# Six float32 products of the identity stand in TensorE's queue among the first scores

## Chip, cores and metric

One core of a Trainium2 chip runs the whole program in one launch. The metric is the device time of one execution in microseconds (us), as the median of the runs. TensorE is called PE here, VectorE DVE, ScalarE ACT, GpSimd POOL, and SP is the queue that issues most of the transfers.

## What is computed

An attention layer with a memory term, and behind it a stack of matrix products. Cut to what matters:

```
B, H, S, D = 4, 8, 576, 64
scores = (q @ k^T) / sqrt(D); causal mask; softmax          # a
local  = a @ v
q_p    = elu(q) + 1
mem    = (q_p @ M_prev) / (q_p . z_prev + 1e-6)
g      = sigmoid(beta) per head
attn   = g * mem + (1 - g) * local
x      = attn as (B*S = 2304, H*D = 512)
out    = ((x @ w1) * (x @ w2)) @ w3 @ w_out                 # 512 -> 1024 -> 1024 -> 512
```

All arrays are float32.

## The kernel before

The attention is worked off in 16 units, each a batch and two heads (`unit_step`). A unit's scores are made in blocks of 128 query rows (`s_all`, line 250; `s_mm0`, line 233), and DVE takes each block out of PSUM, adds the mask and finds the row's extreme in one instruction (`s_red`, line 221). ACT makes the exponentials (`s_exp`, line 265), DVE or ACT scales the rows by their sums (`s_norm`, lines 270 to 278), PE transposes the rows (`t_mm`, line 289), ACT copies them (line 314), and PE multiplies them with v (`pv_mm`, line 326). Line 351 on ACT and line 352 on DVE put the unit's result into the tiles `xs`. The memory term has its own small chain: ACT at lines 172 and 173, DVE at line 179, a product with z (line 181, on DVE in some units and on POOL in others), a sum on DVE (line 189), and a scaling (line 203).

Since nothing stands between `@ w3` and `@ w_out`, the kernel multiplies these two weights with each other first, once. The weights come in as 64-bit words that ACT (line 369) and DVE (lines 373 and 374) turn into float32; the converted tiles are called `wo` (of w_out) and `hh` (of w3). The weight product has eight blocks of 128 rows, each the sum of eight PE products of 128 x 512 (`w_gen`, line 493). Blocks 0 and 1 are made side by side in the two PSUM tiles named `m`; from block 2 on each block takes one of the same two tiles when it is free. A finished block is rounded by ACT into `wH` (line 498), and DVE writes the remainder into `wL` (line 485); after that the PSUM tile is free. So the first product of block 2, which this text calls the third block, waits for the line 485 of block 0. Later the stack of products runs on PE (lines 545 and 566).

The order of the work is written by hand, as the strings in `ORDERS`, one for each unit and one ahead of the first. A word is a step: `ss` and `s0` are the scores, `e0` to `e4` exponentials, `n2` to `n4` normalisations, `ma`, `mv` and `md` the memory term, `gg` the gate of sigmoid values (`gate`), `c` one tick of the weight conversion, `F1` and so on so many weight products. Underneath, a scheduler of the tile framework decides the order in which instructions stand on each engine, by its own idea of how long each takes and of what is ready; the strings give it priorities. An instruction put in at one place can therefore move others far behind it. Each engine works its queue strictly in the order that results.

`warm(n)` can put n transposes of the identity into PE's queue. Before, it is called with n = 0 alone, where it only hands out the PSUM tile of the gate.

Of the kernel before, what the change touches and what calls it, by code (L numbers as in the profile page):

```python
# [20 lines left out]

LOADS = "q0 r1 be r3 n0 r6"
ORDERS = (
    1 * ["ss s0 e2 e1 gg e0 F3 e3 c lq F1 c n3 ma n2 F3 c mv lv lqn F2 md e4 n4 F2"]
    + 1 * ["t1 t2 t3b t4b ma c c ts t4a t3a F1 th pv fin s0 c mb ss e4 c e2 F1 lv F1 e0 F3 c F2 md F3 lq lqn F1 e1 e3 F2 n2 n3 a4"]
    + 1 * ["ma ts t2 t1 t3a t4b th t4a t3b pv fin lv ss e4 e1 s0 mb lq e3 e2 mc n3 lqn e0 a4 n2"]
    + 1 * ["t4b t1 F2 t3b c F2 ma ts th t4a t3a F3 t2 pv mv fin F1 ss e2 c c e3 s0 F1 e1 n3 lqn e4 e0 c md F2 lq lv n2 F2 a4"]
# [14 lines left out]
def attention_moe_kernel(  # L42
# [13 lines left out]
    nc = tc.nc  # L56
# [30 lines left out]
    ident = const.tile([128, 128], F32, name="ident")  # L87
# [27 lines left out]
    def split_qk(p):  # L115
        t = raw_t[p]
        hi = s4_p.tile([128, 2, 640], F32R, tag="s4", name="hi")
        lo = s4_p.tile([128, 2, 640], F32R, tag="s2", name="lo")
        parts_t[p] = hi, lo
        for o, n in ((0, 320), (320, S)):  # L120
            x, y, z = (i[:, :, o:n] for i in (t, hi, lo))
            nc.scalar.activation(out=y, in_=x, func=ACTF.Copy)  # L122
            nc.vector.tensor_tensor(out=z, in0=x, in1=f32(y), op=ALU.subtract)  # L123
# [13 lines left out]
    def load_v(w):  # L137
        p, (c0, c1) = units[w]
        b, h = heads(p)
        t = v_p.tile([128, 2, 4, D], F32, tag="v", name="v")  # L140
        u = v_p.tile([128, 5, 2, D], F32, tag="u", name="u")
        v_t[w] = t, u
        y = v[b, h:h + 2].rearrange("h p k d -> p h k d")
        nc.sync.dma_start(out=t[:, :, 0:c1 - 1], in_=y[:, :, 0:c1 - 1])
        for a in range(2):
            nc.sync.dma_start(out=u[0:64, c0:c1, a], in_=v[b, h + a][0:64, c0:c1])
        m = m_prev[b][:, h:h + 2]
        nc.sync.dma_start(
            out=u[64:128, c0:c1].rearrange("p c a d -> p c (a d)"),
            in_=bass.AP(tensor=m.tensor, offset=m.offset, ap=[[DM, D], [0, c1 - c0], [1, 2 * D]]),  # L150
        )

    def load_qn(w):
        p, (c0, c1) = units[w]
        b, h = heads(p)
        t = qn_p.tile([128, 5, 2, D], F32, tag="qn", name="qn")
        y = qn[b, h // 2]
        nc.sync.dma_start(out=t[64:128, c0:c1], in_=y[0:64, c0:c1])
        k = max(c0, 1)
        nc.sync.dma_start(out=t[0:64, k:c1], in_=y[64:128, k - 1:c1 - 1])  # L160
        if c0 == 0:
            nc.sync.dma_start(out=t[0:64, 0], in_=y[0:64, 0])
        zt = z_p.tile([128, 2, D], F32, tag="z", name="z")
        zs = z_prev[b, h:h + 2]
        nc.sync.dma_start(out=zt, in_=bass.AP(tensor=zs.tensor, offset=zs.offset, ap=[[0, 128], [D, 2], [1, D]]))
        qn_t[w], z_t[w] = t, zt
# [118 lines left out]
    def t_mm(w, what):  # L285
        p, (c0, c1) = units[w]
        pt = pts(w)
        ps = bank()
        tr = lambda o, c, a, kc: nc.tensor.transpose(ps[:, o:o + 128], sm(p, a, c)[:, 128 * kc:128 * kc + 128], ident)  # L289
        if what in ("4a", "4b", "3a", "3b"):  # L290
            c, a = int(what[0]), "ab".index(what[1])
            for kc in range(4):
                tr(128 * kc, c, a, kc)
            s = 256 if c == 4 else 0
            o = 128 if c == 4 else 256
            d = pt[:, a, s:s + 1536].rearrange("p (k q) -> p k q", q=384)[:, :, o:o + 128]
            job = (ps.rearrange("p (k q) -> p k q", q=128), d)
        elif what == "h":
            nc.tensor.transpose(ps[:, 0:128], sm0, ident)
            job = (ps[:, 0:128].rearrange("p (a q) -> p a q", a=2), pt[:, :, SP[0]:SP[0] + 64])  # L300
        else:
            blocks, lo, st, o = {
                "1": (((1, 0), (1, 1)), 0, SP[1], 0),
                "2": (((2, 0), (2, 1)), 0, 384, 128),
                "s": (((2, 2), (4, 4)), 1024, 384, 256),
            }[what]
            here = [i for i, (c, kc) in enumerate(blocks) if c0 <= c < c1]
            k0, k1 = here[0], here[-1] + 1
            for a in range(2):
                for i in here:  # L310
                    tr(256 * a + 128 * i, blocks[i][0], a, blocks[i][1])
            d = pt[:, :, lo:lo + 2 * st].rearrange("p a (k q) -> p a k q", q=st)[:, :, k0:k1, o:o + 128]
            job = (ps.rearrange("p (a k q) -> p a k q", a=2, q=128)[:, :, k0:k1], d)
        nc.scalar.activation(out=job[1], in_=job[0], func=ACTF.Copy)  # L314
# [157 lines left out]
    early = []  # L472

    def warm(n=4):
        if not early:
            early.extend(ps_m.tile([128, DM], F32, tag="m", name="m") for _ in range(2))
        for _ in range(n):
            nc.tensor.transpose(early[0][:, 0:128], ident, ident)
        return early[1]

    def w_gen():
# [136 lines left out]
    def try_tick():  # L618
        if tick[0] <= NJ + 1 and tick_ok():
            conv_tick()  # L620

    def unit_step(w, F):
        p, (c0, c1) = units[w] if w >= 0 else (0, (0, 0))
        nx = w + 1 < NU
        n0, n1 = units[w + 1][1] if nx else (9, 9)
        pn = units[w + 1][0] if nx else NP
        n2 = w + 2 < NU
        here = lambda c: c0 <= c < c1
        then = lambda c: n0 <= c < n1

        ops = dict(
            lqn=(n2, lambda: load_qn(w + 2)),
            lv=(nx, lambda: load_v(w + 1)),
            t4a=(here(4), lambda: t_mm(w, "4a")),
            t4b=(here(4), lambda: t_mm(w, "4b")),
            t3a=(here(3), lambda: t_mm(w, "3a")),
            t3b=(here(3), lambda: t_mm(w, "3b")),
            t2=(here(2), lambda: t_mm(w, "2")),
            t1=(here(1), lambda: t_mm(w, "1")),
            th=(here(0), lambda: t_mm(w, "h")),  # L640
            ts=(w >= 0, lambda: t_mm(w, "s")),
            sh=(nx, lambda: split_qk(pn)),
            ss=(nx, lambda: s_all(w + 1)),
            s0=(then(0), lambda: s_mm0(pn)),
            e4=(then(4), lambda: s_exp(w + 1, 4)),
            e3=(then(3), lambda: s_exp(w + 1, 3)),
            e2=(then(2), lambda: s_exp(w + 1, 2)),
            e1=(then(1), lambda: s_exp(w + 1, 1)),
            e0=(then(0), lambda: s_exp(w + 1, 0)),
            n3=(then(3), lambda: s_norm(w + 1, 2, 4)),  # L650
            n2=(then(0), lambda: s_norm(w + 1, 4, 9)),
            n4=(then(4), lambda: s_norm(w + 1, 0, 2)),
            a4=(then(4), lambda: s_norm(w + 1, 0, 2, True)),
            a3=(then(3), lambda: s_norm(w + 1, 2, 4, True)),
            lq=(n2, lambda: load_qk(w + 2)),
            pv=(w >= 0, lambda: pv_mm(w)),
            fin=(w >= 0, lambda: fin(w)),
            ma=(nx, lambda: mem_a(w + 1)),
            mb=(nx, lambda: mem_b(w + 1, nc.gpsimd)),
            mv=(nx, lambda: mem_b(w + 1, nc.vector)),  # L660
            mc=(nx, lambda: mem_c(w + 1, nc.gpsimd)),
            md=(nx, lambda: mem_c(w + 1, nc.vector)),
            gg=(1, gate),
        )
        for t in ORDERS[w + 1].split():
            if t[0] == "F":
                F.slot(int(t[1:] or 0) * 870)
            elif t == "c":
                try_tick()
            elif t == "d":  # L670
                warm()
            elif ops[t][0]:
                ops[t][1]()

    def gate():
        x = warm(0)[:, 0:H]
        nc.tensor.matmul(x, lhsT=ident[0:1, 0:1].to_broadcast([1, 128]), rhs=beta_sb[0:1], start=True, stop=True)
        nc.scalar.activation(out=g_sb, in_=x, func=ACTF.Exp, scale=-1.0)
        nc.scalar.activation(out=gi, in_=x, func=ACTF.Exp)
        nc.vector.tensor_scalar(out=g_sb, in0=g_sb, scalar1=1.0, scalar2=None, op0=ALU.add)  # L680
        nc.vector.reciprocal(out=g_sb, in_=g_sb)
        nc.vector.tensor_scalar(out=gi, in0=gi, scalar1=1.0, scalar2=None, op0=ALU.add)
        gp = gi.rearrange("p (j a) -> p j a", a=2)
        for k in range(4):
            nc.vector.tensor_copy(out=gis[:, :, 2 * k:2 * k + 2], in_=gp)
        for a in range(2):
            nc.vector.tensor_copy(out=gis[64 * a:64 * a + 64, :, 8], in_=gp[64 * a:64 * a + 64, :, a])
# [18 lines left out]
    for w in range(-1, NC):  # L706
        unit_step(w, F)
# [43 lines left out]
```

## Time and profile before

| | before |
|---|---|
| median of 3 runs | 537.77 us (537.25 to 538.07) |
| profiled execution, its own time | 536.97 us |
| its span, first to last instruction | 535.2 us |
| mean granted clock of PE | 0.997 |
| PE busy | 517.8 us (97%) |
| PE's weight loads busy | 393.9 us (74%) |
| ACT busy | 305.0 us (57%) |
| DVE busy | 289.4 us (54%) |
| POOL busy | 70.5 us (13%) |
| read from HBM | 46.14 MB |

The busy shares are means over the whole span. The start is another thing than the rest: there PE has gaps, the transfer engines are full, and DVE and ACT work without a break. So the stretches of the start are to be read one by one. A granted clock of 1.00 is 2.4 GHz, one of 0.50 is 1.2 GHz.

### The profile page before, as it was taken

How to read it: one execution, taken by the hardware profiler on the slowest of the kernel's cores; microseconds unless marked ns; L12 is line 12 of the kernel's file. 1: busy time of each engine (PE TensorE's matmuls, PEld its weight loads, DVE VectorE, ACT ScalarE, POOL GpSimd, SP SyncE). 2: the span in 40 equal slices, each digit the busy share in tenths (PEclk: the TensorE clock that was granted, in tenths of full speed). 3: DMA queues.
4: the chain of work that ended last, by engine and by line, in shares of the span. 5: the costliest groups of instructions: out<-in, count | busy, mean ns of one | idle time of the engine just before them, and what ended most of it. 6: DMA issues, size and time to landing. Idle time of an engine off the chain costs nothing.

```text
span 535.2 us, 8570 instructions
## 1 busy us (share of the span) xinstructions
PE 517.8 (97%) x3090; PEld 393.9 (74%) x3090; DVE 289.4 (54%) x898; ACT 305.0 (57%) x709; POOL 70.5 (13%) x92
## 2 busy tenths in 40 slices
PE   3999997999999999999999999999999999999997
PEld 2455553557878788778887878787878788888995
DVE  5989789997846476359282758282526111111110
ACT  5689799869567557286575667475747301111121
POOL 1001111000011023001110322010104300114012
PEclk9899999999999999999999999999999999999999
DMA  8998488143303031304030414031210000001001
GB/s 313 417 326 274 116 271 273 39 140 106 116 7 114 14 100 51 129 26 119 8 112 9 130 43 136 23 93 29 61 35 31 35 26 0 0 1 59 21 1 39
DMA packets 34587, 51.40 MB, mean 96 GB/s; under 512 B 13170, under 2 KB 25714, under 8 KB 31986
## 3 DMA queue, kind: packets, MB, share of 16 engines
q1 hardware_dynamic: 34402, 50.74, 29.3%
q8 instruction: 24, 0.39, 0.3%
q14 instruction: 17, 0.14, 0.1%
q10 hardware_dynamic: 144, 0.13, 0.1%
HBM read 46.14 MB, written 4.72 MB: 95 GB/s over the span
## 4 chain that ended last, share of the span: by engine, by line
PE 85%; DVE 6%; ACT 5%; DMA 2%; issue 1%; POOL 0%; SPq 0%; ACTq 0%; DVEq 0%; POOLq 0%
PE m L545 38%; PE m L566 19%; PE x L326 9%; PE s L289 8%; PE s L250 5%; PE m L493 4%; PE sx L250 2%; DMA qn<-qn 1%; ACT s L265 1%; DVE s L221 1%; ACT pt L314 1%; DMA raw<-qkt 1%; ACT wsp L381 1%; DVE sm L221 1%; DVE s L278 1%
## 5 line engine op out<-in xcount | busy, mean ns | idle before, releaser
L545 PE MATMUL m<-xs,wsp 128*128 128x512 f32 (+1 forms) x1008 | 213.4, 365 | 0.0
L545 PEld LDWEIGHTS m<-xs,wsp 128*128 128x128 f32 x1008 | 166.7, 189 | 27.7 <-issue 0.2
L566 PE MATMUL m<-wH,hs 128*128 128x512 f32 x288 | 95.7, 401 | 0.0
L314 ACT ACTIVATE pt<-s 128x512 f32<-128x512 f32 (+1 forms) x128 | 64.0, 558 | 29.2 <-PE s L289 25.2
L265 ACT ACTIVATE s<-s,mx 128x320 f32<-128x320 f32 (+2 forms) x96 | 56.2, 588 | 35.0 <-DVE mx L221 34.9
L527 POOL TENSOR_TENSOR hs<-hh,hs 128x512 fp32r<-128x512 f32 (+1 forms) x41 | 47.6, 1161 | 210.9 <-ACT hs L526 208.9
L554 DVE SCALAR_TENSOR_TENSOR hh<-m,hh 128x512 f32<-128x512 f32 (+1 forms) x40 | 25.5, 637 | 75.5 <-PE m L545 73.8
L493 PE MATMUL m<-wo,hh 128*128 128x512 f32 x128 | 60.4, 616 | 5.0 <-DVE hh L374 4.5
L566 PEld LDWEIGHTS m<-wH,hs 128*128 128x128 f32 x288 | 54.2, 188 | 12.2
L566 PE MATMUL m<-wL,hs 128*128 128x512 f32 x144 | 56.8, 394 | 0.0
L552 ACT ACTIVATE hh<-m 128x512 f32<-128x512 f32 (+1 forms) x40 | 22.0, 551 | 55.9 <-PE m L545 55.5
L493 PEld LDWEIGHTS m<-wo,hh 128*128 128x128 f32 x128 | 23.5, 194 | 31.9 <-issue 23.0
L289 PE MATMUL s<-ident,s 128*128 128x128 f32 x320 | 43.4, 274 | 2.6 <-DVE s L278 1.7
L289 PEld LDWEIGHTS s<-ident,s 128*128 128x128 f32 x320 | 36.7, 140 | 11.1 <-DVE s L278 2.5
L526 ACT ACTIVATE hs<-hh 128x512 fp32r<-128x512 f32 (+1 forms) x41 | 23.7, 577 | 36.5 <-DVE hh L554 18.3
L326 PE MATMUL x<-pt,v 128*64 128x512 f32 (+3 forms) x256 | 38.0, 439 | 0.2 <-ACT pt L314 0.2
L123 DVE TENSOR_TENSOR lo<-raw,hi 128x640 fp32r<-128x640 f32 (+1 forms) x24 | 18.3, 778 | 33.2 <-ACT hi L122 31.6
L352 DVE TENSOR_TENSOR xs<-x,xs 128x576 fp32r<-128x576 f32 (+6 forms) x24 | 13.3, 556 | 42.2 <-ACT xs L351 42.2
L221 DVE CUSTOM_DVE_ANT_0 s<-s,mask 128x320 f32<-128x320 f32 (+1 forms) x64 | 24.4, 420 | 21.9 <-PE sx L250 16.5
L351 ACT ACTIVATE xs<-x 128x576 fp32r<-128x576 f32 (+6 forms) x24 | 11.7, 489 | 39.8 <-PE x L326 35.8
L326 PEld LDWEIGHTS x<-pt,v 128*64 128x64 f32 x256 | 17.0, 136 | 22.3 <-issue 16.6
L581 DVE COPY o<-m 128x512 f32<-128x512 f32 x17 | 11.7, 689 | 37.6 <-PE m L566 37.5
(87 smaller groups left out, 652.6 us busy)
## 6 DMA issues: line engine op xcount, KB each, us to landing
raw<-qkt SPq DMA_DIRECT2D x16, 576.0 KB, 3.9
wst<-w3t SPq DMA_DIRECT2D x8, 1024.0 KB, 9.2
wst<-w SPq DMA_DIRECT2D x8, 1024.0 KB, 8.3
out<-o SPq DMA_DIRECT2D x17, 256.0 KB, 2.0
wst<-w_out SPq DMA_DIRECT2D x4, 1024.0 KB, 10.2
v<-v SPq DMA_DIRECT2D x16, 256.0 KB, 2.8
qn<-qn SPq DMA_DIRECT2D x16, 160.0 KB, 4.0
u<-v SPq DMA_DIRECT2D x32, 80.0 KB, 2.5
```

The source lines that it names most:

```text
L221: nc.vector.tensor_tensor_reduce(out=sm(p, a, c)[:, lo:hi] if c else sm0[:, 0:64], in0=x, in1=mask[:, S - KE[c] + lo:S - KE[c] + hi] if c ...
L250: nc.tensor.matmul(y[a], lhsT=qq[r, 0, 128 * c - 64:128 * c + 64], rhs=kk[r, 1, l:n], start=k == 0, stop=k == len(terms) - 1,)
L265: nc.scalar.activation(out=x, in_=x, func=ACTF.Exp, bias=mx, scale=-1.0, accum_out=sums_of(w)[:, k:k + 1])
L289: tr = lambda o, c, a, kc: nc.tensor.transpose(ps[:, o:o + 128], sm(p, a, c)[:, 128 * kc:128 * kc + 128], ident)
L314: nc.scalar.activation(out=job[1], in_=job[0], func=ACTF.Copy)
L326: nc.tensor.matmul(x[64 * a:64 * a + 64, X0 + lo:X0 + hi], lhsT=vv[:, a, k] if k < 4 else uu[:, k - 4, a], rhs=pt[:, a, o + lo - z:o + hi ...
L493: nc.tensor.matmul(ps, lhsT=w[:, 128 * kc:128 * kc + 128], rhs=wo[:, 512 * (kc % 2):512 * (kc % 2) + 512], start=(kc == 0), stop=(kc == 7))
L526: nc.scalar.activation(out=hs[:, 0, f0:f1], in_=y, func=ACTF.Copy)
L527: nc.gpsimd.tensor_tensor(out=hs[:, 1, f0:f1], in0=y, in1=f32(hs[:, 0, f0:f1]), op=ALU.subtract)
L545: nc.tensor.matmul(ps[:, o:o + k], lhsT=w[:, y, x, j], rhs=xs[j][:, xx, q:q + k], start=(j == order[0] and z == 0), stop=(j == order[-1] a ...
L554: nc.vector.scalar_tensor_tensor(out=hh[:, f, 0:c], in0=ps[:, 0:c], scalar=2.0 ** -8, in1=hh[:, f, 0:c], op0=ALU.mult, op1=ALU.mult)
L566: nc.tensor.matmul(ps, lhsT=hs[:, a, f], rhs=b[f], start=(k == 0), stop=(k == 23))
```

## The change

A word `d6` ahead of the first scores calls `warm(6)`, and `warm` now issues plain float32 products of the identity with itself, 128 x 128 x 128 each, in place of transposes. They write a part of one of the two early PSUM tiles that nobody reads; the first weight product starts that tile afresh. The gate is cut in two steps, `gg` (its product and ACT's two exponentials) and `gh` (DVE's part), which stand next to each other.

```diff
-    1 * ["ss s0 e2 e1 gg e0 F3 ...
+    1 * ["d6 ss s0 e2 e1 gg gh e0 F3 ...
@@ warm
         for _ in range(n):
-            nc.tensor.transpose(early[0][:, 0:128], ident, ident)
+            nc.tensor.matmul(early[0][:, 0:128], lhsT=ident, rhs=ident, start=True, stop=True)
@@ unit_step
             gg=(1, gate),
+            gh=(1, gate_end),
         )
...
-            elif t == "d":
-                warm()
+            elif t[0] == "d":
+                warm(int(t[1:]))
@@ gate
         nc.scalar.activation(out=gi, in_=x, func=ACTF.Exp)
+
+    def gate_end():
         nc.vector.tensor_scalar(out=g_sb, in0=g_sb, scalar1=1.0, scalar2=None, op0=ALU.add)
```

Lines behind 664 move by one, and behind 679 by three. In the built program the six stand behind six score products, since the scheduler moved them, and from there on the order of several engines differs. Three places matter below.

PE's queue at the start of the program, before (`raw` is the first unit's q and k; `s` and `sx` are scores in PSUM; x2 counts equal rows):

```order
L250 MATMUL s<-raw 128x320 x2
L250 MATMUL s<-raw 128x192 x2
L250 MATMUL s<-raw 128x448 x2
L250 MATMUL sx<-raw 128x512 x2
L250 MATMUL s<-raw 128x64 x2
L233 MATMUL s<-raw 64x64 x2
L677 MATMUL m<-beta_sb,ident 128x8
L493 MATMUL m<-wo,hh 128x512 x8
```

The same place now:

```order
L250 MATMUL s<-raw 128x320 x2
L250 MATMUL s<-raw 128x192 x2
L250 MATMUL s<-raw 128x448 x2
L478 MATMUL m<-ident 128x128 x6
L250 MATMUL sx<-raw 128x512 x2
L250 MATMUL s<-raw 128x64 x2
L233 MATMUL s<-raw 64x64 x2
L678 MATMUL m<-beta_sb,ident 128x8
L493 MATMUL m<-wo,hh 128x512 x8
```

The six are ahead of the scores `sx` and all that follows, and behind the first six.

DVE's queue where the second unit's scores are worked off and block 0 of the weight product ends, before (`wL_117` and `wL_118` are `wL` of blocks 0 and 1; rows `L221 ISA mx` write the found extreme):

```order
L221 ISA sm_108,mx<-s,mask 128x448
L221 ISA mx 128x1
L352 TENSOR_TENSOR xs_125<-x,xs_125 128x64
L179 SCALAR_TENSOR_TENSOR qn<-qn,e 128x640
L485 SCALAR_TENSOR_TENSOR wL_117<-m,wH_109 128x512
L485 SCALAR_TENSOR_TENSOR wL_118<-m,wH_110 128x512
L221 ISA s_429,mx<-sx,mask 128x512
```

The same place now:

```order
L179 SCALAR_TENSOR_TENSOR qn<-qn,e 128x640
L270 SCALAR_TENSOR_TENSOR sums<-sums,gis 128x2
L271 RECIPROCAL sums<-sums 128x2
L278 TENSOR_SCALAR sm_108<-sm_108,sums 128x448
L189 TENSOR_REDUCE n<-e 128x10
L221 ISA s_435,mx<-sx,mask 128x512
L221 ISA mx 128x1
L221 ISA s_435,mx<-sx,mask 128x512
L221 ISA mx 128x1
L221 ISA s_435,mx<-s,mask,mx 128x64
L221 ISA mx 128x1
L221 ISA s_435,mx<-s,mask,mx 128x64
```

Next come `L221 ISA mx 128x1` and then the two rows of line 485: these now stand behind a scaling, a sum and four score rows that were behind them.

DVE's queue at the fourth unit, where line 179 releases POOL's product of line 181, before (`wsp` and `wp` are weights of the stack; `s_777` is a tile of scores):

```order
L382 TENSOR_TENSOR wsp<-wp,wsp 128x512
L271 RECIPROCAL sums<-sums 128x5
L271 RECIPROCAL sums<-sums 128x2
L179 SCALAR_TENSOR_TENSOR qn<-qn,e 128x640
L278 TENSOR_SCALAR s_777<-s_777,sums 128x320 x2
L278 TENSOR_SCALAR s_777<-s_777,sums 128x192 x2
L278 TENSOR_SCALAR sm_107<-sm_107,sums 128x64
```

The same line 179 now:

```order
L373 TENSOR_SCALAR wp<-wp 128x512
L374 SCALAR_TENSOR_TENSOR wp<-wst,wp 128x512
L382 TENSOR_TENSOR wsp<-wp,wsp 128x512
L179 SCALAR_TENSOR_TENSOR qn<-qn,e 128x640
L221 ISA s_783,mx<-s,mask 128x320
L221 ISA mx 128x1
L352 TENSOR_TENSOR xs_127<-x,xs_127 128x512
L221 ISA s_783,mx<-s,mask 128x320
```

Line 179 moved ahead of that unit's score rows; the four scalings of line 278 stay behind them, some 40 rows further on. Besides these, near the start one conversion of `hh` on DVE (lines 373 and 374) moved ahead of the first `sx` row, and the second half of that `hh` tile moved five scalings back.

## Rows read from the trace of the kernel before

**Rows 1.** Windows: from:to, length, busy us (instructions) of each engine, PEclk, DMA share, GB/s.

```profile
5.00:10.00 5.00, 4.41 (x26) 2.72 (x22) 3.38 (x13) 3.09 (x11) 0.00 (x0) 1.00 1.00 418
10.00:15.00 5.00, 1.14 (x2) 0.30 (x2) 4.96 (x27) 5.00 (x16) 0.00 (x0) 0.93 0.87 284
15.00:20.00 5.00, 4.44 (x8) 1.76 (x8) 5.00 (x18) 3.57 (x7) 0.00 (x0) 0.73 1.02 429
20.00:25.00 5.00, 5.00 (x17) 2.53 (x17) 5.00 (x11) 1.79 (x4) 0.00 (x0) 1.00 1.00 417
```

**Rows 2.** Chain that ended last, 0 to 60 us: start, length, what.

```profile
19.10 0.67 DVE wo L374
...
19.82 3.70 PE m L493 x8
```

**Rows 3.** A window as in rows 1, of 1 us.

```profile
15.00:16.00 1.00, 1.00 (x2) 0.51 (x2) 1.00 (x5) 1.00 (x3) 0.00 (x0) 0.50 1.03 434
```

**Rows 4.** Timeline of PE: start, length, engine, line, what, count, idle before.

```profile
7.64 1.02 PE L250 MATMUL sx<-raw 64*128 64x512 f32 x4
...
13.86 5.40 PE L493 MATMUL m<-wo,hh 128*128 128x512 f32 x8 [4.45 <-DVE hh L374]
...
15.36 1.91 PE L493 MATMUL m<-wo,hh 128*128 128x512 f32 x2
...
36.47 1.21 PE L326 MATMUL x<-pt,u 128*64 128x128 f32 x20
...
41.85 7.99 PE L493 MATMUL m<-wo,hh 128*128 128x512 f32 x18
```

**Rows 5.** Timeline of DVE, ACT and the queue SP, 9 to 17 us.

```profile
9.03 0.68 DVE L221 CUSTOM_DVE_ANT_0 s<-sx,mask 128x512 f32<-128x512 f32 x1
9.45 0.65 ACT L369 ACTIVATE hh<-wst 128x512 f32<-128x512 f32 x1
16.95 0.33 SPq L445 DMA_DIRECT2D wst<-w3t  x1
```

**Rows 6.** Timeline of DVE and POOL, 32 to 45 us.

```profile
32.58 0.49 DVE L221 CUSTOM_DVE_ANT_0 s<-s,mask 128x320 f32<-128x320 f32 x1 [0.81 <-PE s L250]
...
38.08 0.62 DVE L221 CUSTOM_DVE_ANT_0 sm<-s,mask 128x448 f32<-128x448 f32 x1 [0.51 <-PE s L250]
...
40.37 0.83 DVE L179 SCALAR_TENSOR_TENSOR qn<-qn,e 128x640 f32<-128x640 f32 x1 [0.37 <-ACT e L173]
41.11 1.28 DVE L485 SCALAR_TENSOR_TENSOR wL<-m,wH 128x512 fp32r<-128x512 f32 x2
42.31 0.68 DVE L221 CUSTOM_DVE_ANT_0 s<-sx,mask 128x512 f32<-128x512 f32 x1
...
43.52 0.28 DVE L221 CUSTOM_DVE_ANT_0 s<-s,mask,mx 128x64 f32<-128x64 f32 x1
...
43.94 0.82 DVE L189 TENSOR_REDUCE n<-e 128x10 f32<-128x640 f32 x1
...
46.32 0.45 DVE L278 TENSOR_SCALAR sm<-sm,sums 128x448 f32<-128x448 f32 x1
41.27 1.55 POOL L181 TENSOR_TENSOR e<-qn,z 128x640 f32<-128x640 f32 x1 [39.24 <-DVE qn L179]
```

**Rows 7.** Timeline of DVE and POOL: line 278 alone, and beside POOL's line 181.

```profile
17.53 1.14 DVE L278 TENSOR_SCALAR s<-s,sums 128x320 f32<-128x320 f32 x4
91.62 2.42 DVE L278 TENSOR_SCALAR s<-s,sums 128x320 f32<-128x320 f32 x4
91.92 1.76 POOL L181 TENSOR_TENSOR e<-qn,z 128x640 f32<-128x640 f32 x1 [22.00 <-DVE qn L179]
```

**Rows 8.** PE's waits, 60 to 130 us: for what, us in total, times, longest.

```profile
PE s L289 <- DVE s L278: 1.7, 1, 1.7
PE sx L250 <- DVE xs L352: 1.6, 1, 1.6
PE s L289 <- ACT s L276: 0.8, 2, 0.5
```

More of the change, by code (lines that the diff above doesn't have):

```diff
@@ L23 @@
 ORDERS = (
-    1 * ["ss s0 e2 e1 gg e0 F3 e3 c lq F1 c n3 ma n2 F3 c mv lv lqn F2 md e4 n4 F2"]
+    1 * ["d6 ss s0 e2 e1 gg gh e0 F3 e3 c lq F1 c n3 ma n2 F3 c mv lv lqn F2 md e4 n4 F2"]
     + 1 * ["t1 t2 t3b t4b ma c c ts t4a t3a F1 th pv fin s0 c mb ss e4 c e2 F1 lv F1 e0 F3 c F2 md F3 lq lqn F1 e1 e3 F2 n2 n3 a4"]
```

## The prediction

> **What bounds the kernel now.** Read the windows of the start first [rows 1]. From 5 to 20 us PE is not the bound: between 10 and 15 us it is busy for 1.14 of 5 us, while DVE is busy for 4.96 and ACT for 5.00, and the transfer engines are full (shares of 0.87 to 1.02). The chain of waits says the same: the last DVE piece of it starts at 19.10 and is a conversion of `wo`; from 19.82 the chain is PE alone [rows 2], and PE is busy without a gap, for 5.00 of 5 us from 20 to 25 [rows 1]. The waits of PE from 60 to 130 us are the third thing to read: 1.7 us for line 278 on DVE, 1.6 for `xs` and 0.8 for line 276 [rows 8], 4.1 us in all. So three things can move the end: when PE's dense stretch begins, whether a new gap opens in it, and how much of the later waits a delay is given back from.
>
> PE's clock is low in one place: 0.50, so 1.2 GHz, in the window from 15 to 16 us [rows 3], behind a gap of 4.45 us that ended at 13.86 [rows 4]. The means of 0.93 and 0.73 over 5 us each [rows 1] are 0.7 and 2.7 us at 0.50, so 3.4 us in all.
>
> **The six products.** Each is 128 columns wide. Nine products of 512 columns take 7.99 us at the full clock [rows 4], so 0.89 each, and by the columns 0.22 for one of 128: 1.33 us for six. From below: 20 pieces of 128 columns and less of line 326 take 1.21 us [rows 4], 0.06 each, and the six are twelve such pieces, 0.7 us. From above: at 0.50 one product of 512 columns takes 1.91 us [rows 4], a quarter of it six times is 2.9 us. I take 1.33, as these are the same kind of product with the same full array. They start where `sx` started, at 7.64, so `sx` ends near 10.0 and not at 8.66. Before, that would have hurt, since DVE took `sx` at 9.03 [rows 5]. Now DVE does something else there: a conversion of `hh`, then two blocks of 448, and it comes to `sx` only after 12 us. That covers the 1.33, and the 2.9 too. If DVE were earlier by 2.3 us, it would wait. Cost on the path: 0.
>
> **The early DVE order.** DVE is free at 9.03, and the conversion now standing there needs ACT's line 369, which runs from 9.45 for 0.65 [rows 5]. DVE waits until 10.10, so 1.07 us; the blocks behind it were ready. The second half of that `hh` tile, of about 0.6, stands further back, so the first weight products see only some 0.5 of it. Then DVE is late by 1.07 again, but it has waits of its own: 0.81 at 32.58, 0.51 at 38.08, 0.37 at 40.37 [rows 6], 1.69 together. By 40 us DVE is level. PE, without gaps, stays late by something like 1 to 1.7 us at 42 us, and that is hidden if PE then waits longer anyway (next part). A load on SP waits for the tile that the moved half frees. It went out at 16.95 [rows 5]; now it goes out near 21.5, and all loads on that queue behind it. The transfer engines are at 1.00 until 25 us [rows 1], working off loads issued before, so I cost this at nothing; if that backlog ends first, it is the second rival.
>
> **The third block.** Its first product starts on PE at 41.85 [rows 4], 0.10 after the first line 485 on DVE, which starts at 41.11 and takes half of 1.28 [rows 6]. This is the term that decides. Line 179 ends at 41.11 as before, and it releases POOL's line 181, from 41.27 for 1.55, to 42.82 [rows 6]. DVE now comes to a scaling of line 278 while POOL works. Such a meeting is in the trace: four scalings take 1.14 alone and 2.42 beside POOL's line 181 [rows 7]. So the scaling ends about 0.45 [rows 6] after POOL, at 43.27. Then come line 189 (0.82), the four score rows (42.31 to 43.94, so 1.63), line 485 (0.64) and the 0.10 [rows 6]: 46.46, which is 4.6 later. Rows overlap the next by 0.08 or so, so I take 4.4. Without the meeting, line 189 still waits for POOL: 46.01, so 4.2 at most and 3.8 if DVE's wait of 0.37 at 40.37 goes. From above, 4.6 and one more wait for ACT's exponential of 0.3: 4.9. PE has finished all it can do by then, its earlier lateness included, so 4.4 is the whole delay at this point.
>
> The Trainium skill, "SBUF — State Buffer", "Who interferes with whom", states that DVE and GpSimd share a port pair which one of them locks while the other blocks fully, and that a DVE instruction with one SBUF input outside the two-port modes stays clear of it. The trace agrees, with 2.42 against 1.14 us. By that rule the give-back of the next part is sure; if the meeting were chance instead, 1.28 would not return and the sum would be 3.5.
>
> **What is given back.** In the fourth unit line 179 now stands ahead of the score rows, so POOL's line 181 runs beside these and not beside the scalings. A score row takes 0.68 beside POOL, at 42.31 [rows 6], and 0.68 alone, at 9.03 [rows 5]. The 2.42 become 1.14: 1.28 us of the 1.7 that PE waits there [rows 7, 8]. The other waits are 1.6 and 0.8 [rows 8]. PE comes later, its feeders (ACT's exponentials, `xs`) come later too but by less, as they have slack; against it the new order may open a wait of about 1 us at the second unit's end. Carrying the durations of the rows through the new order leaves 0.9 given back; the ends are 0 and 2.4. Sum: 4.4 - 1.28 - 0.9 = 2.2 us.
>
> **Rivals.**
>
> 1. *All is given back.* PE's delay of 4.4 meets 4.1 us of later waits [rows 8]. If what ends these is set by ACT, DVE and loads that PE's delay does not reach, PE only waits less: 4.4 - 4.1 = 0.3, so 538.1 and not slower by a measurable amount. It decides at the waits for `xs` and for line 278: both must vanish. For it speaks that ACT and DVE have slack after 42 us. Against it, that scores are made by PE itself, so its delay reaches the feeders. Chance 0.16.
> 2. *The loads come late.* The weight tiles behind 21.5 us arrive after the backlog has ended, and nothing but the collision is given back, or not even that: up to 4.4, 542.2. Against it the full shares in rows 1. Chance 0.13.
> 3. *The clock falls in the new gap.* PE stands still from about 42.9 to 46.3. The gap ahead of 13.86 was followed by 0.50 [rows 3, 4]; with the products then taking 1.91 instead of 0.89 [rows 4], about 1.7 us are lost in a stretch like that one. 2.2 + 1.5, so 541.5. Other gaps, of 1.6 and 1.7 us [rows 8], had no fall. Chance 0.13.
> 4. *The products lift the clock and that pays.* The 3.4 us at 0.50 do the work of 1.7 [rows 1]; without them 1.7 us would be saved if PE were the bound there: 536.1. But DVE is the bound [rows 1, 2], and the clock was 1.00 already when `sx` started, so the forecast counts nothing for it. Chance 0.05.
>
> The Trainium skill, "TensorE: Matmul & The Clock Gate", Part 1, states that activity of PE releases the gate and idleness closes it; the 0.50 after the gap agrees. By that rule alone the change helps, which is rival 4.
>
> **How the numbers follow.** The profiled execution took 536.97 us (span 535.2), the median is 537.77, 0.80 above. 536.97 + 2.2 = 539.2 for a profile, and 537.77 + 2.2 = 540.0 for the median. The forecast has a chance of 0.53; its own range is 538.7 to 541.0 (from below 3.8 - 1.7 - 1.2 = 0.9 with half of the 2.4, from above 4.9 - 1.28 - 0.4 = 3.2 with half of the 0.9). The range reaches to most of rivals 1 to 3: 538.0 to 542.3. A measurement of this kernel can tell about 0.2%, 1.08 us, from no change, so 536.7 to 538.8 is the same. Faster: rival 4 and a little of rival 1, 0.07. The same: most of rival 1 and the low end of the forecast, 0.18. Slower: 0.75.
>
> **What would show it.** The six at about 0.22 us each, from 7.6 to 9.0 us. DVE waiting about 1 us near 9 us for ACT's line 369. The third block's first product near 46.3, after a PE gap of some 3.5 us that line 485 ends. Four scalings of the fourth unit at about 1.1 us, and no 1.7 us wait for them. PE's clock at 1.00 from 46 on. The prediction is wrong if DVE reaches line 485 before 43 us, if PE's gap ends later than 47, or if the later waits are nearly gone or unchanged.

## The result, and the profile after

The changed kernel takes 542.18 us (median of 4 runs, 540.94 to 542.53), the kernel before 537.51 us beside it (537.05 to 538.07): a ratio of 1.0081, 95% interval 1.0066 to 1.0096. The profiled execution took 542.15 us, its span is 540.4 us against 535.2. The prediction had the direction and the place right, and 542.18 lies at the top of its range (538.0 to 542.3). That it lies inside, by 0.12, is luck: the same kernel took 542.80 the next time. The likeliest time was 540.0: the loss is about twice what the prediction called likeliest, and more than half of what is missing is a mechanism that it had put aside as a rival.

TensorE (PE) at the start and around the third block, kernel after: start, length, engine, line, what, count of records, idle time before and what ended it.

```profile
4.46 3.57 PE L250 MATMUL s<-raw 64*128 64x320 f32 x12 [4.46 <-DMA raw<-qkt]
7.96 2.41 PE L478 MATMUL m<-ident 128*128 128x128 f32 x12
...
12.10 1.13 PE L493 MATMUL m<-wo,hh 128*128 128x512 f32 x2
16.54 8.03 PE L493 MATMUL m<-wo,hh 128*128 128x512 f32 x14 [3.32 <-ACT e L172]
...
42.32 1.98 PE L493 MATMUL m<-wo,hh 128*128 128x512 f32 x4
46.99 9.69 PE L493 MATMUL m<-wo,hh 128*128 128x512 f32 x18 [2.69 <-DVE wL L485]
...
64.20 1.89 PE L250 MATMUL s<-raw 64*128 64x320 f32 x12
```

The row of 46.99 is the one to set beside the last of [rows 4]. The third block starts at 46.99 and not at 41.85, so 5.14 us later; and its 18 records take 9.69 us and not 7.99, so 1.70 us longer. Windows of the same stretch, kernel after (columns as in rows 1), show why they take longer:

```profile
44.00:46.00 2.00, 0.30 (x1) 0.00 (x0) 2.00 (x6) 1.12 (x3) 0.00 (x0) 1.00 0.97 386
46.00:48.00 2.00, 1.01 (x2) 0.50 (x3) 2.00 (x9) 1.83 (x5) 0.00 (x0) 0.80 1.28 259
48.00:50.00 2.00, 2.00 (x4) 0.84 (x3) 2.00 (x11) 1.96 (x5) 0.00 (x0) 0.50 0.97 309
50.00:52.00 2.00, 2.00 (x5) 0.88 (x4) 2.00 (x5) 0.98 (x2) 0.00 (x0) 0.84 0.72 109
```

PE's granted clock falls to 0.50 (1.2 GHz) right behind the start of the third block. The clock column is the third from the right: 1.00, 0.80, 0.50, 0.84. Behind 52 us it is back at 1.00.

What leads to 46.99 stands in DVE's and POOL's timeline, kernel after:

```profile
10.11 0.43 DVE L373 TENSOR_SCALAR hh<-hh 128x512 uint32<-128x512 uint32 x1 [1.02 <-ACT hh L369]
11.62 0.62 DVE L221 CUSTOM_DVE_ANT_0 sm<-s,mask 128x448 f32<-128x448 f32 x1 [0.35 <-PE s L250]
...
40.83 0.82 DVE L179 SCALAR_TENSOR_TENSOR qn<-qn,e 128x640 f32<-128x640 f32 x1
41.91 1.38 DVE L270 SCALAR_TENSOR_TENSOR sums<-sums,gis 128x2 f32<-128x2 f32 x1 [0.27 <-ACT sm L265]
43.32 0.17 DVE L271 RECIPROCAL sums<-sums 128x2 f32<-128x2 f32 x1
43.52 0.45 DVE L278 TENSOR_SCALAR sm<-sm,sums 128x448 f32<-128x448 f32 x1
43.89 0.81 DVE L189 TENSOR_REDUCE n<-e 128x10 f32<-128x640 f32 x1
44.62 0.68 DVE L221 CUSTOM_DVE_ANT_0 s<-sx,mask 128x512 f32<-128x512 f32 x1
...
46.25 1.28 DVE L485 SCALAR_TENSOR_TENSOR wL<-m,wH 128x512 fp32r<-128x512 f32 x2
41.73 1.54 POOL L181 TENSOR_TENSOR e<-qn,z 128x640 f32<-128x640 f32 x1 [39.69 <-DVE qn L179]
```

Line 485 stands behind the chain of lines 270, 271, 278, 189 and four score rows, as the order said. At the head of that chain an instruction on two columns takes 1.38 us: it ends when POOL's product ends (41.73 + 1.54 = 43.27).

PE's waits from 60 to 130 us, kernel after (for what, us in total, times, longest), answer to [rows 8]:

```profile
PE sx L250 <- DVE xs L352: 1.8, 2, 0.9
PE s L299 <- ACT pt L314: 0.3, 1, 0.3
PE x L326 <- ACT pt L314: 0.2, 1, 0.2
PE s L289 <- ACT s L276: 0.2, 1, 0.2
PE s L289 <- ACT pt L314: 0.2, 1, 0.2
```

By the single waits of the timelines they add up to 2.61 us, and to 4.24 before, the three of [rows 8] and one of 0.17. The wait of 1.7 for line 278 is gone; the others together changed little. So 1.63 us are given back, and the sum closes: 5.14 + 1.70 - 1.63 = 5.21, against 5.2 between the spans (540.4 - 535.2). The medians are only 4.67 apart: the profile of the kernel before is one of its shorter executions.

### The profile page after: what moved, and what is told of

The parts are those of the page before. It is cut to its first block, busy times and chain, and to the rows that moved or that the text cites. A ratio compares the mean times of both kernels' runs of the same rounds, so it can differ in the third digit from the quotient of the medians.

```text
span 540.4 us, 8602 instructions
## 1 busy us (share of the span) xinstructions
PE 522.7 (97%) x3102; PEld 397.9 (74%) x3102; DVE 289.4 (54%) x898; ACT 305.1 (56%) x709; POOL 70.4 (13%) x92
## 4 chain that ended last, share of the span: by engine, by line
PE 85%; DVE 7%; ACT 5%; issue 1%; DMA 1%; DVEq 0%; ACTq 0%
PE m L545 38%; PE m L566 19%; PE x L326 8%; PE s L289 7%; PE m L493 6%; PE s L250 5%; PE sx L250 2%; ACT pt L314 1%; ACT s L265 1%; DVE wo L374 1%; DVE s L221 1%; DMA raw<-qkt 1%; ACT sm L265 1%; PE s L233 1%; DVE s L278 1%
## 5 line engine op out<-in xcount | busy, mean ns | idle before, releaser
L493 PE MATMUL m<-wo,hh 128*128 128x512 f32 x128 | 61.8, 630 | 7.1 <-ACT e L172 3.3
L221 DVE CUSTOM_DVE_ANT_0 s<-s,mask 128x320 f32<-128x320 f32 (+1 forms) x64 | 24.4, 420 | 21.3 <-PE sx L250 16.4
```

The lines of the kernel that those rows point to most:

```text
L221: nc.vector.tensor_tensor_reduce(out=sm(p, a, c)[:, lo:hi] if c else sm0[:, 0:64], in0=x, in1=mask[:, S - KE[c] + lo:S - KE[c] + hi] if c ...
L493: nc.tensor.matmul(ps, lhsT=w[:, 128 * kc:128 * kc + 128], rhs=wo[:, 512 * (kc % 2):512 * (kc % 2) + 512], start=(kc == 0), stop=(kc == 7))
```

## The experiments

Three things could be behind the loss: the six products themselves, the order that the scheduler made around them, or the fall of the clock. All kernels but two are made from the changed kernel, by one edit each; the median of the changed kernel is 542.18.

### The gap filled with products

```diff
-    ... e4 c e2 F1 lv F1 e0 F3 c F2 ...
+    ... e4 c e2 F1 lv F1 e0 F2 z6 F1 c F2 ...
+    def busy(n): # z6: six products of the identity into a scores tile that was read already
+        [nc.tensor.matmul(spot[-1][:, 0:128], lhsT=ident, rhs=ident, start=True, stop=True) for _ in range(n)]
```

The lines that keep that tile in `spot` and that call `busy` at the word `z6` are left out here.

> The changed kernel with six more products of the identity in PE's queue between the last product of blocks 0 and 1 and the first of the third block, so in the gap of 2.69 us ahead of 46.99; nothing else stands elsewhere on any engine. Theory (the gap is set by DVE's line 485, and the fall of the clock behind it costs 1.7 us that the end pays for): the third block still starts at 47.0, PE's clock stays at 1.00 from 44 to 56, the next 18 records of line 493 take 8.0 instead of 9.7, and the time is 540.5 (540.2 to 541.2), 1.0 to 2.0 below the changed kernel's 542.18. Rival (the clock's fall lies under later waits and costs nothing at the end): 542.2, within 0.5. Second rival (the gap's products delay the third block or the clock falls all the same): 542.2 or more, with the third block later than 47.2 or a clock of 0.50 around 48.

Measured: 540.25 us (540.0 to 542.06, 4 runs), ratio to before 1.0065 (1.0047 to 1.0084). PE and windows of this kernel:

```profile
46.62 7.99 PE L493 MATMUL m<-wo,hh 128*128 128x512 f32 x18 [1.35 <-DVE wL L485]
...
78.91 0.33 PE L299 MATMUL s<-ident,sm 128*128 128x128 f32 x1 [1.52 <-ACT pt L314]
```
```profile
46.00:48.00 2.00, 1.38 (x3) 0.68 (x4) 2.00 (x8) 2.00 (x6) 0.00 (x0) 1.00 1.28 251
48.00:50.00 2.00, 2.00 (x6) 0.95 (x5) 2.00 (x10) 1.96 (x5) 0.00 (x0) 1.00 1.02 280
...
80.00:84.00 4.00, 4.00 (x17) 1.93 (x18) 2.74 (x10) 3.95 (x10) 0.00 (x0) 0.57 0.77 261
```

The third block still waits for line 485, the idle time ahead of it is 1.35 instead of 2.69, the clock stays at 1.00, and the 18 records take 7.99 again. The block is not delayed, so the second rival falls. (It starts 0.37 earlier, since the first six products took 2.02 us in this execution and not 2.41, and DVE did not wait for them.) The median is 1.9 us lower, as the theory said. But this run alone does not show that the fall is paid in full at the end. The profiled execution is the slowest of the four (542.06, the others 540.0 to 540.45). In it the clock fell elsewhere: 0.57 in the window from 80 to 84 us, behind a wait of 1.52 us for line 314, where the profile of the changed kernel has one of 0.31. The other three have no trace, and their mean granted clock (0.992 and 0.993) is not above that of the profiled one (0.994). The changed kernel itself took 540.0 in two executions (below). The next run settles it better.

### The second unit's product on DVE

```diff
-    ... pv fin s0 c mb ss e4 ...
+    ... pv fin s0 c mv ss e4 ...
```

> The changed kernel with the second unit's product of line 181 on DVE instead of POOL (mb becomes mv in that unit's string). Theory (POOL's 1.54 from 41.73 blocks DVE's line 270 for 1.38, and through it the four score rows and line 485): without the meeting line 270 takes 0.15 and the product 0.82 on DVE, two steps leave the chain ahead of line 485, the third block starts at 45.6 to 46.2 instead of 46.99, and the gap is 1.3 to 1.9. If a gap of that size leaves the clock alone, as the gaps of 1.56 and 1.71 us of the kernel before did: 539.5 (538.8 to 540.3). If it does not: 541.1. Rival (the third block is late because PE and the conversions are late since the start, whatever POOL does): start at 46.8 or later and 542.2, within 0.5.

Measured: 538.72 us (538.57 to 539.12, 6 runs), ratio 1.0027 (1.0015 to 1.0039). DVE and PE of this kernel:

```profile
41.33 0.83 DVE L181 TENSOR_TENSOR e<-qn,z 128x640 f32<-128x640 f32 x1
42.07 0.15 DVE L270 SCALAR_TENSOR_TENSOR sums<-sums,gis 128x2 f32<-128x2 f32 x1
42.19 0.82 DVE L189 TENSOR_REDUCE n<-e 128x10 f32<-128x640 f32 x1
...
44.55 1.28 DVE L485 SCALAR_TENSOR_TENSOR wL<-m,wH 128x512 fp32r<-128x512 f32 x2
```
```profile
45.30 7.99 PE L493 MATMUL m<-wo,hh 128*128 128x512 f32 x18 [1.35 <-DVE wL L485]
```

Line 270 takes 0.15 us instead of 1.38, though DVE now does 0.83 us more work itself. The third block starts 1.69 us earlier (45.30; expected were 45.6 to 46.2, since the order also put lines 271 and 278 behind line 485), the gap is 1.35, the clock holds. Of the 1.69, 0.37 came in the filled gap too, without this edit: here the six products took 1.91 us. 1.69 + 1.70 = 3.39, and the median is 3.46 lower than that of the changed kernel; the longest execution of the one took 539.12, the shortest of the other, its repeat below included, 539.98. PE's waits from 60 to 130 us add up to 2.38, against 2.61, so they took nothing of it back. The earlier start alone would explain 1.69; so the fall of the clock is paid for at the end, and the first rival of the run above falls. This one word takes away three quarters of the loss with the six products still in place.

### The products behind the scores

```diff
-    "d6 ss s0 e2 ...
+    "ss d6 s0 e2 ...
```

> The same six products, but behind the first unit's scores (ss d6 s0 instead of d6 ss s0). DVE's queue is then that of the kernel before, up to a few rows; on PE some transposes and products change places near 18 us. Theory (the loss is the order, not the products): the products take 1.3 to 2.4 us between 8.8 and 11.5 while PE has nothing else, the third block starts at 42 to 43 with no gap ahead of it, and the time is 538.1 (537.3 to 538.9). Rival (the products' own 2.4 us on PE are what the end pays): 539.9 or more. Rival of the clock (PE's shorter idle stretch ahead of the first weight products keeps the clock at 1.00, and that pays): under 536.8, with no 0.50 between 14 and 18 us; the theory says that DVE bounds that stretch, so that even then nothing is won.

Measured: 538.50 us (538.01 to 539.03, 7 runs), ratio 1.0022 (1.0011 to 1.0033). Windows and PE of this kernel:

```profile
10.00:15.00 5.00, 2.55 (x21) 2.20 (x20) 4.96 (x27) 4.69 (x14) 0.00 (x0) 1.00 0.92 288
15.00:20.00 5.00, 4.30 (x15) 1.78 (x14) 5.00 (x18) 3.59 (x8) 0.00 (x0) 1.00 1.02 431
```
```profile
10.02 1.60 PE L478 MATMUL m<-ident 128*128 128x128 f32 x12
...
42.58 7.99 PE L493 MATMUL m<-wo,hh 128*128 128x512 f32 x18
```

With DVE's queue as before the third block starts at 42.58, without a gap, and the loss is 1.0 us and not 4.7. So the order is what costs, not six products as such. This run also decides rival 4 of the prediction. The clock of the profiled execution is 1.00 throughout the two windows, where [rows 1] has 0.93 and 0.73. It brought nothing: DVE is busy for 9.96 of the 10 us there, and the third block is 0.7 us later than before. That the products hold the clock up is shown for this execution alone: its mean granted clock is 0.999, those of the other six are 0.993 to 0.997, and these took 538.01 to 539.03 us against its 538.70.

### The kernel before with one product on DVE

```diff
-    ... lqn e4 c lq c mb F3 lv F1 a4 F4 ...
+    ... lqn e4 c lq c mv F3 lv F1 a4 F4 ...
```

> The kernel before (no products), with one change: the product of line 181 that runs on POOL at 91.92 beside four scalings of line 278 runs on DVE, behind those scalings. It measures the term of 1.28 us of the prediction by itself. Theory (a lock between POOL's product and DVE's scalings): the four scalings take 1.14 instead of 2.42, PE's wait of 1.71 for them shrinks to about 0.4, DVE gains 0.8 of other work behind it, and the time is 536.2 (535.8 to 536.8). Rival (the meeting was chance, or DVE's additional 0.8 us takes the gain back): 537.5, within 0.5.

Measured: 536.33 us (535.01 to 539.35, 10 runs), ratio 0.9983 (0.9965 to 1.0001). DVE of this kernel, to be set beside [rows 7], and its waits of PE from 60 to 130 us:

```profile
92.29 1.13 DVE L278 TENSOR_SCALAR s<-s,sums 128x320 f32<-128x320 f32 x4
```
```profile
PE sx L250 <- DVE xs L352: 2.2, 1, 2.2
PE s L289 <- ACT s L276: 0.8, 2, 0.5
PE s L289 <- DVE s L278: 0.4, 1, 0.4
PE x L326 <- ACT pt L314: 0.2, 1, 0.2
```

The four scalings take 1.13 us instead of 2.42, and PE's wait for them 0.4 instead of 1.7. So the term of 1.28 is real and no chance. Not all of it arrives: the wait for `xs` is 2.2 instead of 1.6. The medians say 1.2 us; the interval just reaches 1, so at the end the size is less sure than in the trace.

### Transposes instead of products

```diff
-            nc.tensor.matmul(early[0][:, 0:128], lhsT=ident, rhs=ident, start=True, stop=True)
+            nc.tensor.transpose(early[0][:, 0:128], ident, ident)
```

> The changed kernel with six transposes of the identity in place of the six products, at the same place; PE's order of everything else is that of the changed kernel, DVE's differs near the start in some twenty rows (the second half of the conversion of the first hh tile stands behind the first unit's score rows again). It tells the products' own time from the order. Theory (order): PE is done with the first unit's scores a good 1 us earlier, DVE still comes to the third block's line 485 behind the chain that POOL blocks, the third block starts at 46.5 to 47.0 behind a gap of over 2 us, the clock falls to 0.50 behind it, and the time is 541.9 (541.0 to 542.4). Rival (the time that the six take on PE, 2.4 us, is paid at the end): 540.8 or less.

Measured: 541.50 us (539.92 to 542.16, 4 runs), ratio 1.0064 (1.0045 to 1.0083). PE of this kernel:

```profile
8.07 1.06 PE L478 MATMUL m<-ident 128*128 128x128 f32 x6
...
46.61 9.38 PE L493 MATMUL m<-wo,hh 128*128 128x512 f32 x18 [2.67 <-DVE wL L485]
```

The six take 1.06 us instead of 2.41, and the third block starts 0.38 us earlier: that is DVE's wait of 0.35 at 11.62, which is gone, and no more. The filled gap had the same 0.37 with six products of 2.02 us. The gap and the fall of the clock remain. The products' own time is nearly all covered.

### The changed kernel again

> The changed kernel itself once more, beside the same runs of the kernel before as the others here, to have it on the same chip and to see in a second profiled execution whether the clock falls behind the gap near 46 us again. Theory: 542.2 (541.0 to 542.6), third block at 46.6 to 47.2, clock 0.50 behind it. Rival (the fall was an accident of that one execution): no 0.50 near 48 us, and a time about 1.7 us lower.

Measured: 542.80 us (539.98 to 543.62, 6 runs), ratio 1.0078 (1.0053 to 1.0103). PE and DVE of this profile:

```profile
8.00 2.65 PE L478 MATMUL m<-ident 128*128 128x128 f32 x12
11.91 0.62 DVE L221 CUSTOM_DVE_ANT_0 sm<-s,mask 128x448 f32<-128x448 f32 x1 [0.61 <-PE s L250]
...
47.28 9.69 PE L493 MATMUL m<-wo,hh 128*128 128x512 f32 x18 [2.69 <-DVE wL L485]
```

Gap and slow block are there again, to the hundredth. The block starts 0.29 later; the six products took 0.24 longer, and DVE waited 0.26 longer behind them. Two of the six executions took 540.0 us, as much as the kernel with the filled gap. Why is open: they have no trace, and their mean granted clock (0.992 and 0.993) is no higher than that of the profiled execution (0.992) or of those of 543.2 and 543.6 us (0.994). So it does not bear out that the clock stayed up in them.

### Weight products ahead of the second unit's scores

```diff
-    ... t3a F1 th pv fin s0 c mb ss e4 c e2 F1 lv F1 e0 F3 ...
+    ... t3a F3 th pv fin s0 c mb ss e4 c e2 lv e0 F3 ...
```

> The changed kernel with two more weight products ahead of the second unit's scores (t3a F3 ... e4 c e2 lv e0 F3 instead of t3a F1 ... e4 c e2 F1 lv F1 e0 F3). In DVE's queue the first line 485 then stands ahead of the sx rows, line 189 and the scalings; POOL's product stays on POOL. Theory (line 485's place in DVE's queue makes the gap): the third block starts at 43.5 to 45.0, PE's gap ahead of it is under 1.2 us, the clock stays at 1.00 there, and the time is 539.5 (538.5 to 540.8): the late start of 2.4 us remains, and the scalings, now all behind, make a new wait of some 2 us near 75 us. Rival (POOL's lock alone makes the gap, wherever line 485 stands): the third block at 46 or later, and 542.

Measured: 540.74 us (540.09 to 540.85, 4 runs), ratio 1.0052 (1.0038 to 1.0066). DVE and PE of this kernel:

```profile
43.83 0.69 DVE L485 SCALAR_TENSOR_TENSOR wL<-m,wH 128x512 fp32r<-128x512 f32 x1
44.43 0.68 DVE L221 CUSTOM_DVE_ANT_0 s<-sx,mask 128x512 f32<-128x512 f32 x1
```
```profile
44.57 7.99 PE L493 MATMUL m<-wo,hh 128*128 128x512 f32 x18 [0.42 <-DVE wL L485]
...
76.15 1.09 PE L289 MATMUL s<-ident,s 128*128 128x128 f32 x8 [2.32 <-ACT s L276]
```

With line 485 ahead of the score rows the third block starts at 44.57, although POOL's product is still on POOL: its place in DVE's queue makes the gap, as the theory said, and POOL adds to it. But only 1.4 us are saved at the end. The step from 46.99 to 44.57 and the clock are worth 2.4 + 1.7; a new wait of 2.3 us at 76, for the scalings that now stand further back, takes most of the difference. 44.57 is still 2.7 us later than 41.85. That is not the price of the late start alone: 0.42 of it is the gap, and two more weight products now stand ahead of the second unit's scores.

### A version faster than both

The edit is that of the kernel before with one product on DVE, and the same word in the third unit's string (`s0 mb lq` becomes `s0 mv lq`).

> The kernel before with two products of line 181 on DVE instead of POOL, those of the third and of the fifth unit (mb becomes mv in two strings; the run of the fifth alone stood at 536.33). It is what the runs point to as faster than both kernels. Theory (the lock): the wait of PE near 92 us is 0.5 instead of 1.7 us, the one for xs at 83 us gets 0.4 shorter, and the time is 535.4 (534.8 to 536.2). Rival (DVE, busy for 9 of 10 us there, has no 0.8 us to spare): 536.3 to 537.5.

Measured: 536.04 us (535.14 to 536.29, 5 runs), ratio 0.9965 (0.9952 to 0.9978). PE's waits from 60 to 130 us:

```profile
PE s L289 <- ACT s L276: 1.4, 2, 0.9
PE sx L250 <- DVE xs L352: 1.3, 1, 1.3
PE x L326 <- ACT pt L314: 0.2, 1, 0.2
```

The waits add up to 2.9 us instead of 4.2, and the kernel is 1.5 us faster than before, clear of its interval. The expected 535.4 was 0.6 too low: part of the gain turned into a wait for line 276 (1.4 instead of 0.8).

## Why the prediction was half right

**What bounds the start.** Right. DVE bounds it; an execution with PE's clock at 1.00 there was no faster (the products behind the scores).

**The six products.** Their price was 1.33 us; measured were 2.41, near the upper bound of 2.9. They were priced at full speed, since "the clock was 1.00 already when `sx` started", and that was one execution's luck. In the profile before, `sx` did run at full speed at 7.64 (1.02 us). But the twelve records at 4.46 take 3.57 us, and the same twelve take 1.89 at 64.20 in the same trace: the first microseconds run at about half speed though the clock column says 1.00. How long that lasts differs from execution to execution: the same six took from 1.91 us (the second unit's product on DVE) to 2.73 (weight products ahead). The conclusion "cost on the path: 0" held but for 0.35 us: the first blocks of 448 share a PSUM tile with the 64-column pieces that stand behind the products on PE, and DVE's wait at 11.62 ends with these. Where the six took 2.02 or less this wait is gone; where they took 2.65 it is 0.61.

**The early DVE order.** DVE's wait for line 369 is 1.02 (1.07 predicted). That DVE is level by 40 us was wrong: line 179 starts at 40.83 and not 40.37, 0.46 late. For PE the lateness was 1 to 1.7 in the prediction; it finished what it could do at 46.99 - 2.69 = 44.30 and not at 41.85, 2.45 late. Its weight products go on without a break only from 16.54, and from 13.86 before. The second product waits for a conversion of `hh` on DVE, which ends at 16.39 (the profile of 46.99 puts this gap down to line 172, the second profile of the same kernel to line 374 of `hh`). The load that the moved half holds back went out at 21.81, near the predicted 21.5; from 20 to 130 us ACT's waits for loads add up to 1.7 us, against 2.2 before, and PE and DVE have none, so rival 2 did not happen. The lateness of PE cost nothing here, since the gap covered it, as the prediction said it would.

**The third block.** The mechanism was right, but for the instruction that meets POOL. The size was 4.4, measured 5.14: 0.46 from line 179, and about 0.25 because the instruction that POOL blocked was line 270, ahead of the scaling, so that line 271 and the whole scaling still came behind POOL's end.

The Trainium skill, "SBUF — State Buffer", "Who interferes with whom", also names DVE instructions with two SBUF inputs among those that contend with a GpSimd instruction that reads SBUF. Line 270 has two, and the trace agrees: 1.38 us beside POOL, 0.15 without. It is the rule beside the one that the prediction weighed.

**What is given back.** 2.18 in the sum, 1.63 measured. The collision's share came as predicted: the wait of 1.7 is gone, and the four scalings of the fourth unit no longer meet POOL's product. DVE and POOL, kernel after:

```profile
97.83 1.14 DVE L278 TENSOR_SCALAR s<-s,sums 128x320 f32<-128x320 f32 x4
...
87.41 1.55 POOL L181 TENSOR_TENSOR e<-qn,z 128x640 f32<-128x640 f32 x1 [11.19 <-DVE qn L179]
```

Of the 0.9 of other give-back nearly nothing came, since the waits for `xs` and line 314 grew by about what those for line 276 shrank.

**The clock in the new gap.** This is the step that failed: the likeliest sum put the fall of the clock at nothing. It stood as rival 3 with a chance of 0.13, a price of 1.5 us and a time of 541.5, and it happened. Its price in the trace is 1.70 us (9.69 against 7.99), and the run with the second unit's product on DVE shows that the end pays it. The argument against it was that gaps of 1.6 and 1.7 us had no fall; but the gap that the forecast itself predicted was 3.5 us, and the only row near that length was the gap of 4.45 with a fall behind it [rows 3, 4]. By this nearest row the fall should have been in the likeliest case: 2.2 + 1.7 is 3.9, and 541.7 would have been the forecast. Of the signs that the prediction named, "PE's clock at 1.00 from 46 on" did not come, and the gap ended at 46.99, just short of the 47 that it named as its limit (47.28 in the second profile).

## What to carry to other kernels

Before an idle stretch is called covered, look at how long PE stands still in it, and compare that with the gaps in the same trace behind which the clock fell; the work behind such a gap is to be priced at the lower level. An instruction that adds nothing to the path can still cost more than its own length, if a scheduler orders a busy engine anew around it: compare the built queues where one engine releases another's buffer. And where a product on POOL holds up a DVE instruction on the path, try the same product on DVE: 0.83 us of work there was cheaper than 1.54 on POOL. A gain read from one profile is to be held against the spread of the other executions: the changed kernel alone ran from 539.98 to 543.62 us.

## What the runs showed of the hardware

- The clock fell to 0.50 behind gaps of 2.69 us (twice) and 2.67 us (the transposes), and not behind gaps of 1.35 us at the same place (two kernels). At the start it fell in or behind gaps of 3.3 to 4.5 us, and not behind one of 2.45 us in the kernel with the products behind the scores. Later waits of 2.17 us (the kernel before with one product on DVE) and 2.32 us (weight products ahead) had no fall behind them. But once it fell behind a wait of 1.52 us among other short ones (the filled gap, near 80 us). So the length of the last gap alone does not tell it.
- Behind such a gap 18 records of a weight product took 9.69 or 9.38 us instead of 7.99. The executions of the changed kernel alone lie 3.6 us apart (539.98 to 543.62), and their mean granted clocks do not order them.
- At the very start PE ran at about half speed while the clock column said 1.00, for a time that differs between executions: `sx`, at 7.6 to 7.9 us, took 1.02 us in the profile before, and 1.24, 1.81 and 1.92 in the three other runs whose first products are these scores.
- A DVE instruction on 128 x 2 elements was held for 1.23 us by one POOL instruction.
